# Full-height tiles for the last keys, and a gated layer whose product is read where TensorE left it

## Chip, cores and metric

One core of one Trainium2 chip runs the kernel. The metric is device time in microseconds (us) of one launch, the lower the better.

## The reference, cut to what matters

Three layers follow one another, all in float32: sliding-window attention, a gated layer with a three-tap convolution, and a second gated layer with a five-tap one.

```python
# attention: batch 4, 8 heads, 576 positions, 64 wide; window of 128 keys
scores = where((rel >= 0) & (rel < 128), q @ k.T / 8 + bias, -1e9)
attn   = softmax(scores);   x = attn @ v              # -> (4, 576, 512)
# first gated layer, taps over positions k = -1, 0, 1
h = relu(x @ w_in);         g = h * sigmoid(conv3(h)) # 1024 channels
y = g @ w_out                                         # -> (4, 576, 512)
# second gated layer, causal, five taps
gate = sigmoid(conv5(y))
out  = (gate * (y @ w_val)) @ w_out2
```

## The kernel before

Activations stand with channels on the 128 partitions and positions along the free axis. Each batch is cut into two units of positions, u=0 (positions 0 to 253) and u=1 (254 to 575), so there are eight units. A unit goes through `attention` (four pairs of heads) and then through four dense steps: `hidden` (w_in, taps, gate), `mixed` (w_out, the product called y in the reference, and its five taps), `valued` (w_val, times the gate) and `output` (w_out2, to HBM). In order to keep float32 accuracy every operand is split into a high part and a low part, and each dense product is three matmuls: high by high, low by high, high by low (`prod`, lines 693 to 695). A dense group writes one PSUM bank; the ring `ps_m` ("pm" in rows) has four banks, and for the first 16 groups only two of them, because the other two serve the widening of the weights.

In `attention` the product of the probabilities and v (line 653, written to `psx`) works on tiles of 128 keys. The two heads of a pair stand in the two 64-column halves of the array, so matmuls come in pairs, one per head. For u=1 the keys end at 576, so the last tile has only 64 keys: `half` is true there, and `kp` is 64 in place of 128. The value array in HBM is padded with zeros to 640 keys, and the probability tile `p` has its unused places set to zero once. One attention of u=1 has 30 such matmuls: three parts (high by high, high by low, low by high) of five pairs each; one of u=0 has 12. In batch 0 the three parts are issued in two groups (the two parts with high probabilities, then the third), later in one.

In `mixed`, ScalarE (ACT) copies the product from PSUM to an SBUF tile `t` (line 754, a row of line 346), `split` makes the high part (line 337 on ACT or 339 on POOL) and the low part (POOL, line 368), and the first tap is a scaling (line 346 or 347) to a tile `gts`, to which VectorE (DVE) adds four more taps (line 353). In batch 0 one of these is done by ACT (line 363) and POOL (line 364). In `hidden` the taps already read the product from its PSUM bank; rows name them `t<-pm`, those of `mixed` `gts<-t`.

The order of the instructions on each engine is not that of the source. `Program` holds every operation with an estimated duration and a priority, and a list scheduler (`forward`, `backward`, `order`) simulates the five engines seven times and writes out the order of the shortest simulated run. With `bank=` given, it keeps a second engine from an operation on a PSUM bank while another works there; with `port=` it stretches operations of DVE and POOL that overlap. `drain` marks the products with v, after which it adds 85 ns to the next matmul. An estimate that is changed changes the written order everywhere.

Of the kernel before, what the change touches and what calls it, by code (L numbers as in the profile page):

```python
# [7 lines left out]
F32 = mybir.dt.float32  # L8
# [4 lines left out]
AF = mybir.ActivationFunctionType  # L13
ALU = mybir.AluOpType
PSUM = bass.MemoryType.PSUM

B, H, S, D = 4, 8, 576, 64
# [202 lines left out]
def act_t(n, psum=False, ap=0):  # L220
    return n * 0.833 + (50 if psum else 93) + 93 * ap


def dve_t(n, ap=0, fast=False):
    return n * (0.52 if fast else 1.04) + 68 + 61 * ap
# [10 lines left out]
def mm_t(n):  # L236
    return n * 0.444 + 5.0
# [7 lines left out]
def attention_moe_moe_kernel(  # L245
# [14 lines left out]
    nc = tc.nc  # L260
    pg = Program()
# [9 lines left out]
    def st(name, shape, dt):  # L271
        return sb.tile(shape, dt, name=name)
# [15 lines left out]
    cc = st("cc", [128, KF * 3 + KD * 5], F32)  # L288
    c1 = cc[:, 0:KF * 3].rearrange("p (m k) -> p m k", k=3)
    c2 = cc[:, KF * 3:KF * 3 + KD * 5].rearrange("p (m k) -> p m k", k=5)  # L290
# [10 lines left out]
    ring_t = Ring("t", 9, [128, XMAX], F32)  # L301
# [34 lines left out]
    def cast(src, hi, n, prio, reads, writes, mode=None):  # L336
        engs = {"ACT": (act_t(n), lambda: nc.scalar.activation(out=hi, in_=src, func=AF.Copy)),  # L337
                "DVE": (dve_t(n, fast=True), lambda: nc.vector.tensor_scalar(hi, src, 1.0, 0.0, op0=ALU.mult, op1=ALU.add)),
                "POOL": (pool_t(n), lambda: nc.gpsimd.tensor_scalar(hi, src, 1.0, 0.0, op0=ALU.mult, op1=ALU.add))}  # L339
        use = tuple(mode or ('POOL', 'ACT'))  # L340
        pg.add(use, tuple(engs[e][0] for e in use), tuple(engs[e][1] for e in use), prio, reads, writes, port=True)

    def scaled(out, in_, scale, n, prio, reads, writes, engs, psum=False, bank=None):

        ap = 0 if isinstance(scale, float) else 1
        how = {"ACT": (act_t(n, psum, ap), lambda: nc.scalar.activation(out=out, in_=in_, func=AF.Copy, scale=scale)),  # L346
               "DVE": (dve_t(n, ap, fast=not psum), lambda: nc.vector.tensor_scalar(out, in_, scale, None, op0=ALU.mult) if ap
                       else nc.vector.tensor_scalar(out, in_, scale, 0.0, op0=ALU.mult, op1=ALU.add))}
        pg.add(tuple(engs), tuple(how[e][0] for e in engs), tuple(how[e][1] for e in engs), prio, reads, writes,
               bank=bank, port=not psum)  # L350
# [139 lines left out]
    def attention(b, u, p, prio, step):  # L490
# [4 lines left out]
        t0 = k0 // 2  # L495
        tiles = list(range(t0, (j0 + nb - 1) // 2 + 1))
        qk_t, qk = ring_qk.next()
        vr, vrk = V0[p] if V0 and b == u == 0 else ring_vr.next()
        v, vk = ring_v.next()
# [6 lines left out]
        if not (V0 and b == u == 0):  # L506
            sync(lambda: nc.sync.dma_start(
                out=vr[:, 0:nv], in_=vN[b, :, p, t0:t0 + nv, :]),
                early + 11052.0, (), (vrk,), 182.0 * nv)
        half = 128 * (tiles[-1] + 1) > S  # L510
        vkeys = (vrk,)
        vin, v1, v2 = vr[:, 0:nv], v[:, 0, 0:nv], v[:, 1, 0:nv]
        n = 128 * nv
# [19 lines left out]
        if turn:  # L533
            pt, ptk = ring_pt.next()
        groups = [[0, 1], [2, 3]] if nb == 4 else [[0, 1], [2, 3], [4]]
        for gi, g in enumerate(groups):
            gp, sk = ps_s.next()
            a, e = g[0], g[-1] + 1
            pr = prio + step * (e - 1)
# [10 lines left out]
            for i, s, nkey, _ in blk:  # L550
                pg.add("DVE", 128 + 1.05 * nkey, lambda i=i, s=s, nkey=nkey: nc.vector.tensor_tensor_reduce(  # L551
                    out=s, in0=s, in1=bm[:, p, 192 - nkey:192], op0=ALU.add, op1=ALU.min,
                    scale=-0.125, scalar=3.0e38, accum_out=stt[:, 0, i:i + 1]), pr, ("bm",), ((sk, i - a), (stk, 0, i)), bank=sk)
            for i, s, nkey, _ in blk:
                to, tok = s, ()
                if turn:
# [3 lines left out]
                    out=to, in_=s, func=AF.Exp, scale=-1.0, bias=stt[:, 0, i:i + 1],  # L560
# [10 lines left out]
            if turn:  # L571
                slots = []
                for i, s, nkey, _ in blk:
# [14 lines left out]
                s0, sn, st_ = slots[0], len(slots), (slots[1] - slots[0] if len(slots) > 1 else 1)  # L588
# [5 lines left out]
                    out=lo, in0=src, in1=hi, op=ALU.subtract), pr, ((sk, 0), (sk, 1), (ptk, 0, gi)), ((ptk, 1, gi),), bank=sk)  # L594
                continue
            for i, s, nkey, _ in blk:
# [4 lines left out]
                if nth_a in (31,):  # L601
                    t, tk = ring_t.next()
                    t = t[:, 0:nkey]
                    pg.add("ACT", act_t(nkey, True, 1), lambda i=i, s=s, t=t: nc.scalar.activation(
                        out=t, in_=s, func=AF.Copy, scale=stt[:, 2, i:i + 1]), pr, ((sk, i - a), (stk, 2, gi)), (tk,), bank=sk)
                    cast(t, hi, nkey, pr, (tk, "pz" + pk[1:]), ((pk, 0, i),))
                    pg.add("POOL", pool_t(nkey, True), lambda t=t, hi=hi, lo=lo: nc.gpsimd.tensor_tensor(
                        out=lo, in0=t, in1=hi, op=ALU.subtract), pr, (tk, (pk, 0, i), "pz" + pk[1:]), ((pk, 1, i),))
                    continue
                pg.add("ACT", act_t(nkey, True, 1), lambda i=i, s=s, hi=hi: nc.scalar.activation(  # L610
                    out=hi, in_=s, func=AF.Copy, scale=stt[:, 2, i:i + 1]), pr, ((sk, i - a), (stk, 2, gi), "pz" + pk[1:]), ((pk, 0, i),), bank=sk)
                pg.add("DVE", dve_t(nkey, 1), lambda i=i, s=s, hi=hi, lo=lo: nc.vector.scalar_tensor_tensor(  # L612
                    out=lo, in0=s, scalar=stt[:, 2, i:i + 1], in1=hi, op0=ALU.mult, op1=ALU.subtract),
                    pr, ((sk, i - a), (stk, 2, gi), (pk, 0, i), "pz" + pk[1:]), ((pk, 1, i),), bank=sk)
        ca, ce = (1, 8) if u == 0 else (0, 10)
        pr = prio + step * nb
        if not turn:
            pt, ptk = ring_pt.next()
# [14 lines left out]
        mms = []  # L633
        for (pq, pv) in parts:
            for t in tiles:
                for (s0, (so, no), (si, ni), oc, oo, oi) in plan[t]:
                    kp = 64 if (half and t == tiles[-1]) else 128
                    for h in range(2):
                        mms.append((pq, pv, t - t0, s0, so, no, si, ni, oc, oo, oi, kp, h))
        last = {h: max(i for i, m in enumerate(mms) if m[-1] == h) for h in range(2)}  # L640
        first = {h: min(i for i, m in enumerate(mms) if m[-1] == h) for h in range(2)}

        def do_pv(ms):
            r = []
            for i, (pq, pv, ti, s0, so, no, si, ni, oc, oo, oi, kp, h) in ms:
                base = pt[0:kp, pq].rearrange("p a c -> p (a c)")
                lhs = v[0:kp, pv, ti, 64 * h:64 * h + 64]
                o = xp[64 * h:64 * h + 64, :]
                rhs = bass.AP(base.tensor, base.offset + 128 * s0 + 64 * h,
                              [list(base.ap[0])] + [[128 * st_, n_] for st_, n_ in ((so, no), (si, ni)) if n_ > 1] + [[1, 64]])  # L650
                oap = bass.AP(o.tensor, o.offset + oc,
                              [list(o.ap[0])] + [[st_, n_] for st_, n_ in ((oo, no), (oi, ni)) if n_ > 1] + [[1, 64]])
                r.append(nc.tensor.matmul(out=oap, lhsT=lhs, rhs=rhs, start=(i == first[h]), stop=(i == last[h]),  # L653
                                          skip_group_check=True))
            return r

        for gr in ((((0, 0),), ((0, 1),), ((1, 0),)), (((0, 0), (0, 1)), ((1, 0),)), (((0, 0), (0, 1), (1, 0)),))[
                1 if b == 0 else 2]:
            ms = [(i, m) for i, m in enumerate(mms) if m[0:2] in gr]
            dur = sum(64 * m[5] * m[7] / 2.4 + 27 for _, m in ms if m[-1] == 0) + 7  # L660
            rd = tuple((ptk, q, gi) for q in sorted({g[0] for g in gr}) for gi in range(len(groups))) + tuple((vk, q + 1) for q in sorted({g[1] for g in gr}))
            pg.add("PE", dur, lambda ms=ms: do_pv(ms), pr, rd, (xpk,)).drain = True
        x, xk = ring_x.next()
# [9 lines left out]
        else:  # L673
# [3 lines left out]
                out=xl, in0=xp[:, 0:n], scalar=s_dn, in1=xh.bitcast(F32), op0=ALU.mult, op1=ALU.subtract),  # L677
                pr, (xpk, (xk, 0), (sck, 2)), ((xk, 1),))
        xkeys = ((xk, 0), (xk, 1), (xk, 2))
        if u == 1:  # L680
            _, _, pxk, px = X[b, 0, p]
# [27 lines left out]
    def split(src, hi, lo, n, sk, dk, prio):  # L709
        cast(src, hi, n, prio, (sk,), dk[0])  # L710
        sub(src, hi, lo, n, prio, (sk,) + dk[0], dk[1])
# [30 lines left out]
    def mixed(b, u, prio, rate):  # L742

        (g0, g1), (o0, o1) = GR[u], OR[u]
        Ng, No, d = g1 - g0, o1 - o0, o0 - g0
        Y[b, u] = []
        for m in range(KD):
            pr = prio + m * 3 * KF * mm_t(Ng) * rate
            yp, ypk = dense("out", m, G[b, u], Ng, pr)
            y, key = ring_g.next()  # L750
            yf, yk = ring_t.next()
            t, tk = ring_gt.next()
            yh, yl, yk2 = y[:, 0, 0:Ng], y[:, 1, 0:Ng], (((key, 0),), ((key, 1),))
            scaled(yf[:, 0:Ng], yp[:, 0:Ng], 1.0, Ng, pr, (ypk,), (yk,), ('ACT',), True)
            split(yf[:, 0:Ng], yh, yl, Ng, yk, yk2, pr)
            scaled(t[:, 0:No], yf[:, d:d + No], c2[:, m, 4:5], No, pr, (yk, "cc"), (tk,), ('ACT', 'DVE'))
            for k in range(3, -1, -1):
                lo_ = 4 - k if o0 == 0 else 0
                tap(t[:, lo_:No], yf[:, d + lo_ + k - 4:d + No + k - 4], c2[:, m, k:k + 1], No, pr, (yk, "cc"), tk,
                    k in ((3,) if b == 0 else ()))  # L760
            pg.add("ACT", act_t(No), lambda t=t: nc.scalar.activation(out=t[:, 0:No], in_=t[:, 0:No], func=AF.Tanh, scale=0.25),
                   pr, (), (tk,))
            Y[b, u].append((yh[:, d:d + No], yl[:, d:d + No], yk2[0] + yk2[1], t, tk))
        return prio + KD * 3 * KF * mm_t(Ng) * rate
# [49 lines left out]
    for p in range(NP):  # L814
        attention(0, 0, p, p * T0 / NP, T0 / NP / 5)
# [10 lines left out]
    def attentions(b, u, base, T):  # L826
        nb = len(BLK[u])
        for p in range(NP):
            attention(b, u, p, base + T * (p / NP * 0.72 + 0.081), T * 0.72 / NP / (nb + 1))
# [12 lines left out]
    t, todo = T0, UNITS  # L842
    for i, (b, u) in enumerate(todo):
        base = t
        for f in steps:
            t = f(b, u, t, rate)
# [84 lines left out]
```

## Time and profile before

| what | us |
|---|---|
| three timed runs, median (lowest to highest) | 459.61 (458.53 to 460.18) |
| the profiled execution, its own time | 460.59 |
| span of its trace, first to last instruction | 458.8 |
| TensorE (PE) busy | 444.5 (97%) |
| VectorE (DVE) busy | 351.8 (77%) |
| ScalarE (ACT) busy | 323.9 (71%) |
| GpSimd (POOL) busy | 247.8 (54%) |

The profiled execution lies 1.8 us above its span, and 1.0 us above the median. Busy time is the time in which at least one instruction of the engine was under way. The durations of matmuls overlap, so that their cost is read from the starts of two that follow one another, not from the duration of one. The granted TensorE clock is 1.0 in all of the span.

### The profile page before, as it was taken

The page shows a single profiled execution, that of the slowest core. Times are in us where ns is not written, and L with a number is a line of the kernel's source. Part 1 is how long each engine was busy: PE and PEld are TensorE (multiplying, and loading weights), DVE is VectorE, ACT ScalarE, POOL GpSimd, SP SyncE. Part 2 cuts the span into 40 slices and gives each one's busy share as a digit, 9 for nine tenths or more (in the row PEclk, how much of TensorE's full clock was granted, in tenths as well). Part 3 has the DMA queues.
Part 4 walks back from the last instruction along what each step waited for, and adds up shares of the span by engine and source line. Part 5 has one row for each costly group of instructions (what it writes and reads, how often), then busy time and mean ns, then how long its engine had stood idle before and what let it go on. Part 6 is the DMA issues. An engine that isn't in the chain of part 4 may idle for free.

```text
span 458.8 us, 10275 instructions
## 1 busy us (share of the span) xinstructions
PE 444.5 (97%) x3585; PEld 416.4 (91%) x3585; DVE 351.8 (77%) x1019; ACT 323.9 (71%) x938; POOL 247.8 (54%) x402
## 2 busy tenths in 40 slices
PE   7988999999999999999999999999999999999996
PEld 6767889988999999999999999998999999989996
DVE  5798998897997768885979487956968687936490
ACT  3988999865986568675975587766856687657532
POOL 2787889992567426340665337351753266654532
PEclk9999999999999999999999999999999999999999
DMA  8766666339643436558172427293426547460001
GB/s 271 264 221 217 212 209 214 99 94 317 146 102 60 105 89 150 116 118 182 52 131 72 108 87 164 74 183 98 68 55 136 131 106 145 81 105 1 1 1 58
DMA packets 75236, 57.86 MB, mean 126 GB/s; under 512 B 55984, under 2 KB 65968, under 8 KB 75184
## 3 DMA queue, kind: packets, MB, share of 16 engines
q1 hardware_dynamic: 75184, 57.21, 48.5%
q8 instruction: 28, 0.46, 0.4%
q14 instruction: 24, 0.20, 0.1%
HBM read 39.10 MB, written 4.72 MB: 96 GB/s over the span
## 4 chain that ended last, share of the span: by engine, by line
PE 43%; DVE 18%; ACT 13%; DMA 9%; POOL 6%; issue 3%; SPq 0%; ACTq 0%; POOLq 0%; DVEq 0%
PE pm L693 12%; PE pm L694 12%; PE pm L695 11%; DVE gts L353 7%; PE pss L547 4%; PE psx L653 4%; DMA pt<-p 3%; DMA raw<-in_w_out 3%; DVE t L353 2%; POOL g L368 2%; DMA vr<-in_vN 2%; ACT pss L559 2%; ACT p L610 1%; ACT sg L390 1%; ACT t L346 1%
## 5 line engine op out<-in xcount | busy, mean ns | idle before, releaser
L368 POOL TENSOR_TENSOR g<-t,g 128x254 fp32r<-128x254 f32 (+1 forms) x96 | 80.7, 842 | 25.5 <-ACT g L337 21.1
L353 DVE SCALAR_TENSOR_TENSOR gts<-t,cc,gts 128x322 f32<-128x322 f32 (+4 forms) x120 | 78.4, 682 | 10.4 <-ACT gts L346 8.7
L693 PE MATMUL pm<-x,win 128*128 128x256 f32 (+1 forms) x256 | 80.6, 315 | 1.1 <-DVE t L353 0.6
L693 PE MATMUL pm<-g,wout 128*128 128x254 f32 (+1 forms) x256 | 79.7, 311 | 0.0
L694 PE MATMUL pm<-x,win 128*128 128x256 f32 (+1 forms) x256 | 76.2, 298 | 0.2 <-DVE x L676 0.2
L694 PE MATMUL pm<-g,wout 128*128 128x254 f32 (+1 forms) x256 | 76.2, 298 | 0.0
L695 PE MATMUL pm<-g,wout 128*128 128x254 f32 (+1 forms) x256 | 75.8, 296 | 0.0
L695 PE MATMUL pm<-x,win 128*128 128x256 f32 (+1 forms) x256 | 75.8, 296 | 0.0
L353 DVE SCALAR_TENSOR_TENSOR t<-pm,cc,t 128x325 f32<-128x325 f32 (+3 forms) x112 | 56.0, 513 | 11.6 <-ACT t L346 9.0
L339 POOL TENSOR_SCALAR g<-t 128x254 fp32r<-128x254 f32 (+1 forms) x55 | 26.1, 474 | 69.0 <-DVE t L353 34.1
L551 DVE CUSTOM_DVE_ANT_0 pss<-pss,bm 128x192 f32<-128x192 f32 (+2 forms) x144 | 47.8, 337 | 16.3 <-PE pss L547 14.6
L547 PE MATMUL pss<-qk 128*128 128x192 f32 (+2 forms) x288 | 57.6, 323 | 2.6 <-DVE pt L593 2.6
L693 PEld LDWEIGHTS pm<-x,win 128*128 128x128 f32 x256 | 48.2, 188 | 4.4 <-DVE t L353 2.3
L559 ACT ACTIVATE pss<-pss,st 128x192 f32<-128x192 f32 (+2 forms) x108 | 40.6, 376 | 15.3 <-DVE st L551 14.0
L693 PEld LDWEIGHTS pm<-g,wout 128*128 128x128 f32 x256 | 48.2, 188 | 1.4 <-DVE t L353 0.3
L547 PEld LDWEIGHTS pss<-qk 128*128 128x128 f32 x288 | 44.8, 193 | 5.0 <-DVE pt L593 4.5
L612 DVE SCALAR_TENSOR_TENSOR p<-pss,st,p 128x192 f16<-128x192 f32 (+2 forms) x103 | 36.5, 386 | 16.1 <-DMA pt<-p 10.8
L694 PEld LDWEIGHTS pm<-x,win 128*128 128x128 f32 x256 | 48.3, 189 | 0.4 <-DVE x L676 0.4
L695 PEld LDWEIGHTS pm<-g,wout 128*128 128x128 f32 x256 | 48.6, 190 | 0.0
L694 PEld LDWEIGHTS pm<-g,wout 128*128 128x128 f32 x256 | 48.5, 190 | 0.0
L695 PEld LDWEIGHTS pm<-x,win 128*128 128x128 f32 x256 | 48.2, 188 | 0.0
L346 ACT ACTIVATE t<-pm 128x254 f32<-128x254 f32 (+2 forms) x64 | 25.8, 409 | 26.9 <-PE pm L695 26.9
(109 smaller groups left out, 1184.9 us busy)
## 6 DMA issues: line engine op xcount, KB each, us to landing
qk<-in_qk SPq DMA_DIRECT2D x16, 544.0 KB, 3.8
qk<-in_qk SPq DMA_DIRECT2D x16, 384.0 KB, 3.6
raw<-in_w_out SPq DMA_DIRECT2D x12, 512.0 KB, 4.2
raw<-in_w_in SPq DMA_DIRECT2D x8, 512.0 KB, 4.4
vr<-in_vN SPq DMA_DIRECT2D x16, 256.0 KB, 2.9
raw<-in_vN SPq DMA_DIRECT2D x8, 384.0 KB, 4.5
out<-t SPq DMA_DIRECT2D x16, 161.0 KB, 1.9
raw<-in_w_val SPq DMA_DIRECT2D x4, 512.0 KB, 3.9
```

The costliest lines, as they stand in the source:

```text
L339: "POOL": (pool_t(n), lambda: nc.gpsimd.tensor_scalar(hi, src, 1.0, 0.0, op0=ALU.mult, op1=ALU.add))}
L346: how = {"ACT": (act_t(n, psum, ap), lambda: nc.scalar.activation(out=out, in_=in_, func=AF.Copy, scale=scale)), "DVE": (dve_t(n, ap, fast ...
L353: pg.add("DVE", dve_t(n, 0 if isinstance(scalar, float) else 1), lambda: nc.vector.scalar_tensor_tensor(out=out, in0=in0, scalar=scalar, i ...
L368: "POOL": (pool_t(n, True), lambda: nc.gpsimd.tensor_tensor(out=lo, in0=src, in1=hi.bitcast(F32), op=ALU.subtract))}
L547: return [nc.tensor.matmul(out=o, lhsT=q_t[:, i, :], rhs=k_t[:, kc:kc + nkey], start=True, stop=True, skip_group_check=True) for i, o, nke ...
L551: pg.add("DVE", 128 + 1.05 * nkey, lambda i=i, s=s, nkey=nkey: nc.vector.tensor_tensor_reduce(out=s, in0=s, in1=bm[:, p, 192 - nkey:192], ...
L559: pg.add("ACT", act_t(nkey, True, 2), lambda i=i, s=s, to=to: nc.scalar.activation(out=to, in_=s, func=AF.Exp, scale=-1.0, bias=stt[:, 0, ...
L612: pg.add("DVE", dve_t(nkey, 1), lambda i=i, s=s, hi=hi, lo=lo: nc.vector.scalar_tensor_tensor(out=lo, in0=s, scalar=stt[:, 2, i:i + 1], in ...
L653: r.append(nc.tensor.matmul(out=oap, lhsT=lhs, rhs=rhs, start=(i == first[h]), stop=(i == last[h]), skip_group_check=True))
L693: return [nc.tensor.matmul(out=o, lhsT=wh, rhs=hi, start=first, stop=False), nc.tensor.matmul(out=o, lhsT=wh, rhs=lo, start=False, stop=Fa ...
L694: nc.tensor.matmul(out=o, lhsT=wh, rhs=lo, start=False, stop=False),
L695: nc.tensor.matmul(out=o, lhsT=wl, rhs=hi, start=False, stop=last)]
```

## The change

Two edits are made in the body of the kernel, and the durations that the scheduler is told follow them. First, the last tile of keys is multiplied at its full height of 128 rows: `half` and `kp` go, and the 64 upper rows hold the padding's zeros. Second, `mixed` no longer copies y out of PSUM. ACT casts the high part directly from the bank, DVE (no longer POOL) subtracts it from the bank's content for the low part, and the scaling and the taps read the bank, which therefore stays taken until the last tap.

```diff
-        half = 128 * (tiles[-1] + 1) > S
...
-                    kp = 64 if (half and t == tiles[-1]) else 128
...
-                base = pt[0:kp, pq].rearrange("p a c -> p (a c)")
-                lhs = v[0:kp, pv, ti, 64 * h:64 * h + 64]
+                base = pt[:, pq].rearrange("p a c -> p (a c)")
+                lhs = v[:, pv, ti, 64 * h:64 * h + 64]
...
-            dur = sum(64 * m[5] * m[7] / 2.4 + 27 for _, m in ms if m[-1] == 0) + 7
+            dur = sum(64 * m[5] * m[7] / 2.4 + 2 for _, m in ms if m[-1] == 0) + (120 if len(gr) > 1 else 60)
...
-            yf, yk = ring_t.next()
+            yf, yk = yp, ypk
...
-            scaled(yf[:, 0:Ng], yp[:, 0:Ng], 1.0, Ng, pr, (ypk,), (yk,), ('ACT',), True)
-            split(yf[:, 0:Ng], yh, yl, Ng, yk, yk2, pr)
-            scaled(t[:, 0:No], yf[:, d:d + No], c2[:, m, 4:5], No, pr, (yk, "cc"), (tk,), ('ACT', 'DVE'))
+            pg.add("ACT", act_t(Ng, True), lambda yf=yf, yh=yh: nc.scalar.activation(out=yh, in_=yf[:, 0:Ng], func=AF.Copy),
+                   pr, (yk,), yk2[0], bank=yk)
+            scaled(t[:, 0:No], yf[:, d:d + No], c2[:, m, 4:5], No, pr, (yk, "cc"), (tk,), ('ACT', 'DVE'), True, yk)
+            pg.add("DVE", dve_t(Ng), lambda yf=yf, yh=yh, yl=yl: nc.vector.tensor_tensor(
+                out=yl, in0=yf[:, 0:Ng], in1=yh.bitcast(F32), op=ALU.subtract), pr, (yk,) + yk2[0], yk2[1], bank=yk)
...
                 tap(t[:, lo_:No], yf[:, d + lo_ + k - 4:d + No + k - 4], c2[:, m, k:k + 1], No, pr, (yk, "cc"), tk,
-                    k in ((3,) if b == 0 else ()))
+                    k in ((3,) if b == 0 else ()), yk)
```

## Rows read from the trace of the kernel before

**Rows 1.** The page's engine table: busy us, share of span, instructions.

```profile
PE 444.5 (97%) x3585; PEld 416.4 (91%) x3585; DVE 351.8 (77%) x1019; ACT 323.9 (71%) x938; POOL 247.8 (54%) x402
```

**Rows 2.** Three stretches: busy us (instructions) of PE, PEld, DVE, ACT, POOL; granted clock.

```profile
60.00:90.00 30.00, 29.56 (x266) 27.08 (x266) 27.13 (x66) 29.77 (x76) 28.61 (x40) 1.00 0.53 179
180.00:210.00 30.00, 30.00 (x289) 28.56 (x289) 23.18 (x71) 19.56 (x61) 11.14 (x21) 1.00 0.61 131
210.00:240.00 30.00, 30.00 (x232) 28.21 (x231) 24.59 (x80) 24.44 (x75) 13.73 (x22) 1.00 0.49 110
```

**Rows 3.** PE's waits, longest first: us in total, times, longest us.

```profile
PE pss L547 <- DVE pt L593: 2.6, 6, 0.8
```

**Rows 4.** Line 653's matmuls by shape: busy us, mean ns.

```profile
L653 PE MATMUL psx<-pt,v 64*64 64x64 f16 x96 | 10.4, 213 | 0.0
...
L653 PE MATMUL psx<-pt,v 128*64 128x64 f16 x96 | 9.4, 193 | 0.0
```

**Rows 5.** PE in order of time around one product with v of u=1.

```profile
191.19 1.62 PE L653 MATMUL psx<-pt,v 128*64 128x128 f16 x30
192.75 0.39 PE L693 MATMUL pm<-g,wout 128*128 128x254 f32 x1
```

**Rows 6.** The same product: line 653's matmuls started by each window's end.

```profile
190.99:191.28 0.29, 0.09 (x4) 0.09 (x6) 1.00 0.00 0
190.99:191.39 0.40, 0.20 (x6) 0.20 (x8) 1.00 0.00 0
190.99:191.45 0.46, 0.26 (x8) 0.26 (x8) 1.00 0.00 0
190.99:191.57 0.58, 0.38 (x10) 0.31 (x10) 1.00 0.00 0
190.99:191.72 0.73, 0.53 (x12) 0.42 (x12) 1.00 0.00 0
```

**Rows 7.** PE in order of time around one product with v of u=0.

```profile
254.10 0.69 PE L653 MATMUL psx<-pt,v 128*64 128x256 f16 x12
254.72 0.42 PE L693 MATMUL pm<-g,wo 128*128 128x322 f32 x1
```

**Rows 8.** The last u=1 product, after a late weight load, counted as in rows 6.

```profile
409.80:411.21 1.41, 1.28 (x25) 1.10 (x27) 1.00 0.70 233
409.80:411.29 1.49, 1.36 (x28) 1.18 (x28) 1.00 0.71 240
```

**Rows 9.** The page's costliest groups: busy us, mean ns, idle before.

```profile
L368 POOL TENSOR_TENSOR g<-t,g 128x254 fp32r<-128x254 f32 (+1 forms) x96 | 80.7, 842 | 25.5 <-ACT g L337 21.1
L353 DVE SCALAR_TENSOR_TENSOR gts<-t,cc,gts 128x322 f32<-128x322 f32 (+4 forms) x120 | 78.4, 682 | 10.4 <-ACT gts L346 8.7
L353 DVE SCALAR_TENSOR_TENSOR t<-pm,cc,t 128x325 f32<-128x325 f32 (+3 forms) x112 | 56.0, 513 | 11.6 <-ACT t L346 9.0
L339 POOL TENSOR_SCALAR g<-t 128x254 fp32r<-128x254 f32 (+1 forms) x55 | 26.1, 474 | 69.0 <-DVE t L353 34.1
L346 ACT ACTIVATE t<-pm 128x254 f32<-128x254 f32 (+2 forms) x64 | 25.8, 409 | 26.9 <-PE pm L695 26.9
```

**Rows 10.** Single forms: busy us, mean ns, idle before.

```profile
L593 DVE TENSOR_TENSOR pt<-pss,pt 128x512 f16<-128x512 f32 x12 | 8.2, 680 | 0.4 <-ACT pt L591 0.4
...
L593 DVE TENSOR_TENSOR pt<-pss,pt 128x256 f16<-128x256 f32 x8 | 3.3, 416 | 0.1
```

**Rows 11.** Batch 0's first `mixed` (u=0): ns least, median, most; first and last start.

```profile
L695 PE MATMUL pm<-g,wout x32: 277/280/284, 70.5 to 85.9; 128*128 128x254 f32 x32
```

**Rows 12.** The last unit's end in order of time: DVE, then POOL [its idle time].

```profile
442.01 1.01 DVE L347 TENSOR_SCALAR gts<-t,cc 128x322 f32<-128x322 f32 x1
442.94 2.87 DVE L353 SCALAR_TENSOR_TENSOR gts<-t,cc,gts 128x322 f32<-128x322 f32 x6
...
446.60 1.37 DVE L776 SCALAR_TENSOR_TENSOR gts<-gts,pm 128x322 f32<-128x322 f32 x3
...
446.80 2.57 POOL L368 TENSOR_TENSOR g<-gts,g 128x322 fp32r<-128x322 f32 x3 [3.96 <-ACT g L337]
```

More of the change, by code (lines that the diff above doesn't have):

```diff
@@ L636, in attention @@
                 for (s0, (so, no), (si, ni), oc, oo, oi) in plan[t]:
-                    kp = 64 if (half and t == tiles[-1]) else 128
                     for h in range(2):
-                        mms.append((pq, pv, t - t0, s0, so, no, si, ni, oc, oo, oi, kp, h))
+                        mms.append((pq, pv, t - t0, s0, so, no, si, ni, oc, oo, oi, h))
         last = {h: max(i for i, m in enumerate(mms) if m[-1] == h) for h in range(2)}
@@ L644, in do_pv @@
             r = []
-            for i, (pq, pv, ti, s0, so, no, si, ni, oc, oo, oi, kp, h) in ms:
-                base = pt[0:kp, pq].rearrange("p a c -> p (a c)")
-                lhs = v[0:kp, pv, ti, 64 * h:64 * h + 64]
+            for i, (pq, pv, ti, s0, so, no, si, ni, oc, oo, oi, h) in ms:
+                base = pt[:, pq].rearrange("p a c -> p (a c)")
+                lhs = v[:, pv, ti, 64 * h:64 * h + 64]
                 o = xp[64 * h:64 * h + 64, :]
```

## Prediction

> **What bounds the kernel now.** I read the engine table first: TensorE is busy for 444.5 us of the 458.8, the next engine, DVE, for 351.8 [rows 1]. A busy share can hide overlap, so the stretches come next. From 180 to 240 us PE is busy in every one of the 60 us, while DVE, ACT and POOL rest for a fifth to over a half of it [rows 2]. Then the list of PE's waits: its longest entry is 2.6 us in all, over 6 waits [rows 3]. So outside the start, what is cut from PE's own issue is cut from the time, as long as the others keep up. The stretch from 60 to 90 us is different: ACT is busy for 29.77 and POOL for 28.61 of 30 us, so there it is as much these two that set the pace [rows 2].
>
> **Part one, the 64-row tile.** There are 96 matmuls of 64 rows [rows 4]: two heads by three parts in each of the 16 attentions of u=1. What one costs shows only in starts. Within a part, the pairs have 128, 256, 128, 64 and 64 columns, the last being the 64-row one. Reading the counts, the second pair has started by 191.28, the third by .39, the fourth by .45, the 64-row pair by .57 and the next part's first by .72 [rows 6]. So 256 columns took 0.11 us and 128 took 0.06, which is columns streaming; but the step into the 64-row pair took 0.12 and the step out of it 0.15, both after only 64 columns, for which a quarter of 0.11, or 0.03 us, would do. The first pair of the product, after a dense matmul, is also late in passing on: it starts at 191.19 [rows 5] and the second by .28, so 0.08 to 0.09 for 128 columns where a settled pair takes 0.06. I read the array as being emptied whenever the height of the tile changes, twice per part. A product of u=0, which has no such tile, puts 12 matmuls into 0.62 us [rows 7]; that of u=1 needs 1.56 us for 30 [rows 5].
>
> What the full-height pair will cost no row shows, and it is bounded from both sides. Below, its columns alone: 0.03 us. Above, its weights: where weights came late, three matmuls followed in 0.08 us one by one, 0.027 us each, whatever their columns [rows 8], and a pair has two loads, so 0.055 to 0.06. For the 12 products of batches 1 to 3, with three steps in and two steps out inside the product and two late first pairs spared: at the upper price 3 x (0.12 - 0.06) + 2 x (0.15 - 0.06) + 2 x 0.02 = 0.40 us; at the lower 3 x 0.09 + 2 x 0.12 + 0.04 = 0.55. The four products of batch 0 are issued in two groups, with one step out inside: 0.18 + 0.09 + 0.02 = 0.29, or 0.27 + 0.12 + 0.02 = 0.41. In all 12 x 0.40 + 4 x 0.29 = 6.0 us, or 12 x 0.55 + 4 x 0.41 = 8.2. I take 6.4, near the end that the weights give, since [rows 8] is the same instruction and narrow pairs cannot hide two loads behind so few columns.
>
> The Trainium skill speaks against this edit: TensorEngine Tiling (Array Packing), section "When to Use Tiling", has a contraction of 64 rows or fewer use two row tiles, which may double the speed. By that the sum of this part would be zero or a loss. The trace does not agree: here the partner tile is never used, and the 64-row pair is among the slowest steps of the product.
>
> **Part two, y stays in PSUM.** There are 32 tiles (8 units by 4). ACT: the copy (409 ns mean) [rows 9] becomes a cast of the same size from the same bank, so no change; the second pass for the high part goes, from ACT or from POOL (474 ns there) [rows 9]. POOL: 32 of 96 subtractions of 842 ns go [rows 9], 27 us in all, and with its share of casts some 35 of its 247.8. DVE: the 32 subtractions come to it. The nearest rows are tensor_tensor from PSUM at 416 ns for 256 columns and 680 for 512 [rows 10], so about 0.42 for the 254 columns of u=0 and 0.49 for the 326 of u=1: 14.5 us more. But the 120 taps change their source. From SBUF they take 682 ns, from PSUM, in `hidden`, 513 [rows 9]: 120 x 0.17 = 20 us less. DVE comes out some 6 us lighter. None of this is on PE's path, so I price it at nothing where PE is the bound; its cover is that DVE rests 5 to 7 us in each 30 [rows 2].
>
> A rule would turn that around. The Trainium skill, VectorE: DVE Perf Modes, section "Rules for kernel authors", advises to copy a matmul's output to SBUF first when many operations follow. Weighed against rows: the slow taps from SBUF are those that ran while POOL worked. At the end of the last unit POOL sat idle for the 3.96 us before 446.80, and there six taps took 2.87 us, 0.48 each [rows 12]. By the rule, with every SBUF tap at 0.48, the change would make DVE 120 x 0.03 + 14.5 = 18 us heavier. By rows 9, which are the mean over the whole run, it is 6 us lighter. I go by rows 9.
>
> At the end this matters. From 442 us DVE works with hardly a pause until the last gate product [rows 12], and PE's `output` waits for what follows. Two or so subtractions of 0.49 come into this queue; the scaling that took 1.01 us there [rows 12] would be near the 0.51 of a PSUM tap. I put this at +0.3 us, between -0.5 and +1.0.
>
> What is queued longer is the bank. Before, it was free after one copy of 0.41 us [rows 9]. After, it is held for the cast 0.41, the subtraction 0.42 to 0.49, the scaling about 0.5 and four taps of 0.51: 3.4 to 3.5 us plus hand-overs. With four banks the next write to it comes three groups later. One group of the first `mixed` takes (85.9 - 70.5) / 4 = 3.9 us [rows 11], so three are over 11 us: the hold is covered. But for the first 16 groups there are two banks, and the slack is one group, 3.9 us. Batch 0's extra ACT and POOL step (one SBUF addition on POOL, 0.84 like the subtraction) in the middle of the taps takes 0.4 more than the tap it replaces and two more hand-overs, so the hold reaches about 4 us there, just the slack. What stalls is the third and fourth group of `mixed` and the first two of `valued`: 0 to 1 us each, so 0 to 4. Against that stands relief in the same stretch, where POOL and ACT were full: 4 x 0.84 us of subtractions and four casts of 0.47 go, 5 us of work off two crowded engines, of which at most half is on the path. I take -0.5 for this stage, between +4 and -2.5.
>
> **Sum.** -6.4 + 0.3 - 0.5 = -6.6. The profiled execution of 460.59 us would become 454.0; it was 1.0 above the median of the runs, 459.61, which becomes 453.0.
>
> **Rivals.** (1) Part of what PE gains is given back: the freed time shows a wait on DVE or ACT, which are 5 to 10 us from full in each 30 [rows 2]. For: a list-scheduled order is written anew everywhere. Half of part one lost leaves -3.4: 456.2. Chance 0.16. (2) Relief pays more than I count: columns alone set the narrow pairs (8.2) and the crowded start gains 2.5: -10.4, or 449.2. Chance 0.08. (3) Slower: the bank's hold decides. If DVE serves taps late, each of the 32 groups keeps PE from its next bank. From 0.2 us each the gain of 6.4 is gone; at 0.4 us each the kernel is 32 x 0.4 - 6.6 = 6.2 slower: 465.8. Against: three groups of slack outside the start, and `hidden` already works from its banks with half the matmuls per group. Chance 0.05. (4) The change of height is not the reason, and narrow pairs are simply slow: every 64-column pair in the trace stands next to a change of height, so no row separates them. Then part one is worth nothing and the time is 459.4, no change. Against: the pair after the step out is late by 0.02 to 0.03 again, as after a dense matmul, which width does not explain. [...] Chance 0.06.
>
> **How the numbers follow.** The forecast, -4.5 to -9.0 with 453.0 as its middle, has 0.65. The likeliest case's own range is 450.6 to 455.1. For eight in ten the range takes in rival (1) and most of (2): 449.5 to 456.8. A measurement of this kernel can tell about 0.3%, 1.4 us, from no change. Faster: 0.65 + 0.16 + 0.08 = 0.89; same: rival (4), 0.06; slower: 0.05.
>
> **What would show it.** No 64-row matmuls in line 653; a u=1 product that lasts 1.1 to 1.2 us in place of 1.56; taps of `mixed` named gts<-pm at about 0.51 us; POOL near 213 us and DVE near 346 busy; PE busy about 438. Part one is wrong if the narrow pairs still step at 0.12 or more. Part two is wrong if PE shows waits of over 3 us in total on DVE or ACT operations on a pm bank, above all between 70 and 100 us, or if the last unit ends more than 1 us later after its last `mixed` matmul than before.

## Result

The changed kernel takes 455.37 us (median of 4 runs, 454.31 to 455.83) against 459.52 (458.53 to 460.18): ratio 0.9902, 95% interval 0.9878 to 0.9927. It is 4.2 us faster; the prediction was 453.0, 6.6 faster. The result lies 0.3 us above the likeliest case's own range (450.6 to 455.1) and inside the wider one (449.5 to 456.8). The profiled execution is the fastest of the four, 454.31, with a span of 452.5 (before 458.8), so the two traces stand 6.3 us apart, more than the medians.

The page of the changed kernel, its engine table, to be held against [rows 1]:

```profile
PE 436.9 (97%) x3605; PEld 412.1 (91%) x3605; DVE 342.7 (76%) x1056; ACT 319.9 (71%) x930; POOL 201.9 (45%) x341
```

PE is still the busiest engine, with 7.6 us less. DVE lost 9.1 us and POOL 45.9.

PE in order of time around a product with v of u=1, the counterpart of [rows 5]:

```profile
190.44 1.04 PE L651 MATMUL psx<-pt,v 128*64 128x128 f16 x30
191.41 0.76 PE L546 MATMUL pss<-qk 128*128 128x192 f32 x3
```

Thirty matmuls pass in 0.97 us; before it was 1.56. The same product as in [rows 6], with the matmuls started by each window's end in the first bracket and the weight loads in the second:

```profile
190.24:190.64 0.40, 0.20 (x6) 0.20 (x8) 1.00 0.90 361
190.24:190.69 0.45, 0.25 (x8) 0.25 (x10) 1.00 0.92 369
190.24:190.72 0.48, 0.28 (x10) 0.28 (x12) 1.00 0.91 365
190.24:190.75 0.51, 0.31 (x12) 0.31 (x14) 1.00 0.86 343
```

The third pair has started by 190.64, the fourth by .69, the fifth by .72 and the sixth, the next part's first, by .75. So the step after 128 columns takes 0.05 us and a step after 64 columns 0.03, and the steps of 0.12 and 0.15 are gone. The loads show what a change of height did: here two loads are always ahead of the matmuls, while in [rows 6] none is ahead at the step into the 64-row pair (8 and 8) or at the step out of it (10 and 10). The groups of line 651 by shape, as in [rows 4]:

```profile
L651 PE MATMUL psx<-pt,v 128*64 128x64 f16 x192 | 10.9, 194 | 0.0
```

No 64-row form is left; its 96 matmuls have joined the 96 of 128 rows and 64 columns. And the page's groups for the second edit, against [rows 9]:

```profile
L368 POOL TENSOR_TENSOR g<-t,g 128x254 fp32r<-128x254 f32 (+1 forms) x64 | 51.9, 814 | 28.2 <-ACT g L337 25.5
...
L353 DVE SCALAR_TENSOR_TENSOR gts<-pm,cc,gts 128x322 f32<-128x322 f32 (+4 forms) x120 | 57.2, 506 | 0.1
```

The 120 taps take 506 ns each from PSUM, 682 before from SBUF, and a third of POOL's subtractions has gone to DVE, where the forms show:

```profile
L755 DVE TENSOR_TENSOR g<-pm,g 128x326 fp32r<-128x326 f32 x16 | 7.8, 489 | 5.2 <-ACT gts L346 4.3 <-ACT g L752 0.9
...
L755 DVE TENSOR_TENSOR g<-pm,g 128x254 fp32r<-128x254 f32 x16 | 6.6, 410 | 0.0
```

### The profile page after: what moved, and what is told of

It is laid out like the page before. It is cut to its first block, busy times and chain, and to the rows that moved or that the text cites. A ratio compares the mean times of both kernels' runs of the same rounds, so it can differ in the third digit from the quotient of the medians.

```text
span 452.5 us, 10277 instructions
## 1 busy us (share of the span) xinstructions
PE 436.9 (97%) x3605; PEld 412.1 (91%) x3605; DVE 342.7 (76%) x1056; ACT 319.9 (71%) x930; POOL 201.9 (45%) x341
## 4 chain that ended last, share of the span: by engine, by line
PE 59%; DVE 15%; ACT 13%; DMA 7%; issue 4%; POOL 1%; SPq 0%; DVEq 0%; ACTq 0%; POOLq 0%
PE pm L691 17%; PE pm L692 15%; PE pm L693 15%; PE pss L546 5%; DVE gts L353 4%; PE psx L651 4%; DMA pt<-p 3%; DVE t L353 2%; ACT sg L390 2%; DMA raw<-in_w_in 2%; DVE pss L550 1%; ACT pss L558 1%; PE pss L584 1%; ACT pm L392 1%; DMA raw<-in_w_val 1%
## 5 line engine op out<-in xcount | busy, mean ns | idle before, releaser
L368 POOL TENSOR_TENSOR g<-t,g 128x254 fp32r<-128x254 f32 (+1 forms) x64 | 51.9, 814 | 28.2 <-ACT g L337 25.5
L563 POOL TENSOR_SCALAR st<-st 128x2 f32<-128x2 f32 (+1 forms) x56 | 11.1, 199 | 103.6 <-ACT pss L558 87.8
L353 DVE SCALAR_TENSOR_TENSOR gts<-pm,cc,gts 128x322 f32<-128x322 f32 (+4 forms) x120 | 57.2, 506 | 0.1
L611 DVE SCALAR_TENSOR_TENSOR p<-pss,st,p 128x192 f16<-128x192 f32 (+1 forms) x103 | 36.4, 386 | 12.8 <-DMA pt<-p 9.0
L609 ACT ACTIVATE p<-pss,st 128x192 f16<-128x192 f32 (+1 forms) x103 | 35.9, 403 | 14.0 <-DMA pt<-p 10.2
```

What stands on the lines that cost most here:

```text
L353: pg.add("DVE", dve_t(n, 0 if isinstance(scalar, float) else 1), lambda: nc.vector.scalar_tensor_tensor(out=out, in0=in0, scalar=scalar, i ...
L368: "POOL": (pool_t(n, True), lambda: nc.gpsimd.tensor_tensor(out=lo, in0=src, in1=hi.bitcast(F32), op=ALU.subtract))}
L563: "POOL": (165, lambda a=a, e=e: nc.gpsimd.tensor_scalar(stt[:, 2, a:e], stt[:, 1, a:e], 1e-9, 1.0 / PSC, op0=ALU.add, op1=ALU.mult))}
```

## Experiments

The changed kernel has three things in it: the height of the tile, y in PSUM, and a new estimate for the scheduler. Twelve kernels took them apart. All ratios are against runs of the kernel before on the same chip. The scheduler simulates seven orders (passes) and writes out the one with the shortest simulated span; "passes" below are counted from one, and the simulated span is the scheduler's own number.

| kernel | height | PSUM | estimate | pass, simulated us | median us | ratio (95%) |
|---|---|---|---|---|---|---|
| before | | | old | 4th, 434.2 | 459.4 (459.1 to 459.7 by chip) | 1 |
| e1 | x | | old | 4th, 434.2 | 453.95 | 0.9890 (0.9871 to 0.9909) |
| e2 | x | | new | 7th, 432.5 | 461.63 | 1.0059 (1.0036 to 1.0081) |
| e3 | | x | old | 2nd, 434.6 | 458.08 | 0.9971 (0.9953 to 0.9989) |
| e4 | x | x | old | 2nd, 434.6 | 452.62 | 0.9853 (0.9825 to 0.9881) |
| changed | x | x | new | 7th, 432.5 | 455.37 | 0.9902 (0.9878 to 0.9927) |
| e5 | x | x | new | 3rd, 433.4 | 455.54 | 0.9911 (0.9882 to 0.9941) |
| e6 | x | x | new | 2nd, 436.9 | 458.10 | 0.9960 (0.9941 to 0.9979) |
| e7 | | | old | 7th, 434.6 | 463.98 | 1.0096 (1.0071 to 1.0121) |
| e8 | x | x | old in batch 0 | 2nd, 433.2 | 454.55 | 0.9894 (0.9867 to 0.9922) |
| e9 | x | | old | 7th, 434.6 | 457.33 | 0.9965 (0.9950 to 0.9981) |
| e10 | x | x | old | 5th, 438.9 | 460.41 | 1.0027 (1.0009 to 1.0046) |
| e11 | x | x | new | 6th, 433.3 | 453.68 | 0.9895 (0.9877 to 0.9913) |
| e12 | x | | old | 5th, 435.7 | 459.98 | 1.0021 (1.0001 to 1.0042) |

Before and e1, e3 and e4, e7 and e9 are pairs in which every engine gets the same operations in the same order; within a pair only the height differs.

**e1, the height alone.**

```diff
-                    kp = 64 if (half and t == tiles[-1]) else 128
+                    kp = 128
```

> The kernel before with the last key tile at 128 rows and nothing else; the scheduler is told the old durations, so the order of every engine is that of before. Theory A (PE's issue is the bound after the start, and the height change is all of the gain): the 12 products of batches 1 to 3 fall from 1.76 us of PE time, start to start, to 1.18, so 7.0 us, and those of batch 0 give at most 1.9 more in a start that other engines bound: 452 to 453 us, 1.4 to 1.6% faster. Theory B (y in PSUM carries some of the gain): less than 3 us faster here, 456.5 or more. Theory C (the order has to be written anew to use the freed time): within 1.4 us of before.

Measured: 453.95 us, 1.1% faster. Its product with v, in PE's order of time:

```profile
189.20 1.04 PE L653 MATMUL psx<-pt,v 128*64 128x128 f16 x30
190.17 0.39 PE L693 MATMUL pm<-g,wout 128*128 128x254 f32 x1
```

0.97 us again. So the height by itself is worth about 5 us, a little less than theory A said. That is no less than the whole change gave (the two intervals overlap). Theories B and C in their plain form fall.

**e2, the height and the new estimate.**

```diff
-            dur = sum(64 * m[5] * m[7] / 2.4 + 27 for _, m in ms if m[-1] == 0) + 7
+            dur = sum(64 * m[5] * m[7] / 2.4 + 2 for _, m in ms if m[-1] == 0) + (120 if len(gr) > 1 else 60)
```

> As the height alone, and the scheduler is told the new, shorter duration of the products with v, so the order is written anew. Theory A: the estimate changes the order but not the work, within 1 us of the height alone. Theory C: the new order is worth 2 us or more, either way.

Measured: 461.63, which is 7.7 us slower than e1 with the same work. All of e1's gain is lost to the order that the new estimate led to. Theory C holds in its second form: the order matters, here against the kernel.

**e3, y in PSUM alone**, the part of the diff in `mixed`, and nothing else.

> The kernel before with y kept in PSUM for the cast, the low part and the taps; the last key tile keeps its 64 rows and the estimate of the products is the old one. Theory A: DVE and POOL are off PE's path, so no difference, within 1.4 us of before. Theory B: faster by 1.5 to 4 us. The theory that the held banks give part of the gain back: slower by 2 to 3 us, with PE waiting on DVE or ACT operations on pm banks.

Measured: 458.08, 0.3% faster, at the edge of what can be told from no change; theory A's band just holds. No loss to held banks is seen: PE waits 0.8 us in all for the taps of `mixed` on a pm bank. But its order is another one too, so this number alone does not price the edit.

**e4, both edits under the old estimate.** The changed kernel with the old line for `dur`.

> The changed kernel with the old estimate for the products with v (27 ns per pair and 7, in place of 2 and 120 or 60). Theory A: within 1 us of the changed kernel, 454.5 to 456.5. Theory C: the estimate is worth 2 us or more.

Measured: 452.62, 1.5% faster than before and 2.3 us (by ratio) to 2.8 us (by median) faster than the changed kernel; theory A's band is missed. It has the lowest median of all kernels here. Against e3, its pair, the ratio falls by 0.0118, 5.4 us: the height's gain again. The start shows where it stands. Each fence is the last group of matmuls of unit 0's `output`, with the first and last start at the end of the line; kernel before, then the changed one, e3 and e4:

```profile
L695 PE MATMUL pm<-g,wo x16: 277/280/283, 98.3 to 108.1; 128*128 128x254 f32 x16
```

```profile
L693 PE MATMUL pm<-g,wo x16: 278/280/284, 99.7 to 107.9; 128*128 128x254 f32 x16
```

```profile
L695 PE MATMUL pm<-g,wo x16: 277/280/283, 98.8 to 105.4; 128*128 128x254 f32 x16
```

```profile
L693 PE MATMUL pm<-g,wo x16: 277/280/283, 97.5 to 104.1; 128*128 128x254 f32 x16
```

In e4 unit 0's last matmul starts 4.0 us earlier than before, in the changed kernel 0.2. What follows it takes 346.0 us in the trace of e4 (span 450.1) and 344.6 in that of the changed kernel (452.5). So the whole loss of the changed kernel's order against that of e4 stands in the start.

**e5, e6, e7, e11: the same kernel in another pass.** The edit, with i = 2, 1 and 5 in the changed kernel and 6 in the one before:

```diff
-            if best is None or span < best[0]:
+            if i == 2:
```

> The changed kernel, but the order written out is that of the third of the scheduler's seven simulated passes (433.4 us by its own simulation) in place of the shortest, the last (432.5). Work, shapes and estimates are the same. Theory L (the scheduler's choice among nearly equal orders is a draw, worth several us on the chip): the three passes of the changed kernel run so far and now spread over 3 us or more, and not in the order of their simulated spans. Theory S (the short estimate makes any order worse, the start above all): within 1.5 us of the changed kernel, unit 0's last matmul at 107 us or later.

> As the one before with the second pass (436.9 us by the scheduler's own simulation, 4.4 longer than the one it chose). Theory L: anywhere from 452 to 459. Theory S: slower than the changed kernel, as simulated.

> The kernel before with the order of the scheduler's last pass (434.6 us by its own simulation, 0.4 longer than the one it chose). Theory L: 1.5 us or more from before, either way. Theory S: within 1 us of before, as the simulation has it.

> The changed kernel in the order of the sixth pass (433.3 us by the scheduler's own simulation). Theory L: within 452 to 458.5, as the other three passes of it. A theory that the kept PSUM bank is worth some 3 us over a mean of orders: 455 or so.

Measured: the changed kernel in four of its orders takes 453.68, 455.37, 455.54 and 458.10; the kernel before in two of its own 459.4 and 463.98, though the simulation sees 0.4 us between these.

Theory L is missed by e5 and e6, which with the changed kernel spread over 2.7 us and follow the simulated spans; only e7 bears it out. Theory S is missed too: e7 is 4.5 us from before, unit 0's last matmul starts at 106.5 us in e5 (106.1 in e11), and not every order under the short estimate is worse, since e10, under the old one, is slower than all four. e6 is slower than the changed kernel, as it asked. e11 lies in theory L's band, and 1.3 us below the 455 of the theory about the bank. By ratio e11, the changed kernel and e5 (0.9895, 0.9902, 0.9911), which the simulation puts within 1 us, cannot be told apart.

Wherever kernels of the same operations and the same estimate differ by more than the noise, the shorter simulated span is the faster one on the chip: before and e7; e1, e9 and e12; e4 and e10; the changed kernel and e6. What the simulation has wrong is the size: 0.4 us became 4.4 (before, e7) and 3.4 (e1, e9), all by ratio, and 4.2 became 6 to 8 (e4, e10). Between two estimates its spans did not compare here: 432.5, the shortest, belongs to e2 and to the changed kernel alike, and each is slower than its counterpart under the old estimate (e1 with 434.2, e4 with 434.6).

PE's waits in e7, as in [rows 3], without the one of 2.1 us at the start that before has too:

```profile
PE pss L585 <- DVE dg L577: 2.1, 4, 0.9
PE pm L693 <- DVE t L353: 1.9, 3, 0.9
...
PE pm L694 <- POOL g L368: 1.3, 3, 0.7
```

No one wait stands out: several of 1 to 2 us in total, for DVE, POOL and (1.4) ACT, have come in place of the one of 2.6 and shorter ones of before.

**e8, the old estimate in batch 0 alone.**

```diff
-            if best is None or span < best[0]:
+            if i == 1:
...
+            if b == 0:
+                dur = sum(64 * m[5] * m[7] / 2.4 + 27 for _, m in ms if m[-1] == 0) + 7
```

> The changed kernel with the old estimate for the products of batch 0 alone and the order of the second pass, the one that the changed kernel under the old estimate took everywhere; so the order of the start is that of the run with the old estimate, and the later units are ordered under the new one. If the loss to the new estimate sits in the order of the start: unit 0 ends at 104 to 105 us as there, and the whole takes 452 to 453.5. If it sits in the later units: 455 or more with the early start.

Measured: 454.55, between the two bands. Unit 0's last matmul starts at 105.3 us in its trace, later than the 104.1 of e4, and what follows takes 347.5 us, more than in the changed kernel (344.6) under the same estimate. So this is one more order, and it doesn't divide the changed kernel's loss.

**e9, e10, e12: more orders.** e9 is e7 with `kp = 128`; e10 is e4 and e12 is e1, each with i = 4.

> The order of the kernel before's last pass, which took 464.0 us, with the height of the last key tile changed and nothing else. If the height's gain does not depend on the order: 5 to 6 us off that, 458 to 459, as in the two pairs that have one order each (before against the height alone, the PSUM edit against the changed kernel under the old estimate), 5.5 us both. If a worse order swallows it: 461 or more.

> Both edits under the old estimate, in the order of the fifth pass (438.9 us by the scheduler's own simulation; the second pass, 434.6, took 452.6 on the chip). Theory L (a draw): anywhere from 452 to 458, so less than the 4.3 us that the simulation says may show. If the simulation is right: 456.5 or more.

> The height alone under the old estimate in the order of the fifth pass (435.7 us by the scheduler's own simulation), the counterpart without y in PSUM. If the PSUM edit is worth some 3 us over a mean of orders: 456 to 461, slower than most kernels with it. If it is worth nothing: as often below 455 as above.

Measured: e9 takes 457.33, a little below its band; its ratio is 0.0131 below that of e7, 6.0 us, so the height's gain is seen in a slow order as well. e10 takes 460.41, outside of what theory L gave it: here the simulation was right, that this order is over 4 us worse than that of e4. (In eight of e10's twelve runs the granted clock was 0.993 to 0.996; the four at 1.0 have a median of 459.1, which alters nothing in this.) e12 takes 459.98, in the band of a PSUM edit worth 3 us, which one order can't prove.

With the height edit, the seven orders with y in PSUM have a mean ratio of 0.9920 (0.9853 to 1.0027), the four without it 0.9984 (0.9890 to 1.0059). The difference, 0.0064 or 2.9 us, is smaller than either spread, so it is a hint and no more.

## Why the prediction came out as it did

**Right: what bounds the kernel, and the mechanism of part one.** PE's issue is cut and the time follows. In three pairs of one order the height gives 5.1, 5.4 and 6.0 us (ratios 0.9890; 0.9971 to 0.9853; 1.0096 to 0.9965, times 459.4), each known to 0.9 to 1.5 us. Rival (4), that narrow pairs are slow by themselves, fell: the full-height narrow pairs step in 0.03 us. The Trainium skill says in TensorEngine Tiling (Array Packing), section "Key Properties", that changing the tiling mode drains the array. The trace agrees that the change costs: with one height left in the product, 0.12 and 0.15 us became 0.03. No run puts two 64-row pairs next to each other, so what such a pair costs by itself is not shown.

**Mis-sized: the price of a narrow pair.** The prediction took the end that late weights give, 0.055 to 0.06 us, and with it 0.40 us per product. Measured, it is 0.58 us (1.55 to 0.97, medians of the 12 in before and e1), a little more than columns alone give (0.55). That makes 12 x 0.58 = 7.0 us. In batch 0 the first group went from 1.04 to 0.69 us and the second from 0.52 to 0.40, so 4 x 0.46 = 1.8, where 0.29 each had been put: 8.8 in all instead of 6.4. The step that failed is the reading of [rows 8]. With 25 to 28 matmuls started by 411.21, .24, .26 and .29, those of one head are 0.05 apart (25 and 27, 26 and 28), which is the settled step for 128 columns; the 0.027 us came from the two heads running out of step, and is no price of a load. The Trainium skill, in TensorE: Matmul & The Clock Gate, section "Step-by-step: what each phase is for", has weight loads pulled ahead of matmuls in flight. The counts agree: in the settled product two loads are ahead at every step.

**Counted, but not paid: batch 0.** Of 8.8 us, 5 to 6 arrive. Where the rest went shows when the traces of a pair of one order are laid over each other. The first edited product, the first of batch 1 with u=1, and the first after batch 2's, each in before and then in e1:

```profile
57.91 1.11 PE L653 MATMUL psx<-pt,v 128*64 128x128 f16 x20
56.81 0.76 PE L653 MATMUL psx<-pt,v 128*64 128x128 f16 x20
...
181.45 1.62 PE L653 MATMUL psx<-pt,v 128*64 128x128 f16 x30
180.02 1.04 PE L653 MATMUL psx<-pt,v 128*64 128x128 f16 x30
...
330.72 0.69 PE L653 MATMUL psx<-pt,v 128*64 128x256 f16 x12
324.76 0.69 PE L653 MATMUL psx<-pt,v 128*64 128x256 f16 x12
```

e1 is 1.1 us ahead where both kernels have run the same instructions, which is chance. Over batch 0 it gains 0.3 of the 1.8 us saved there, over batches 1 and 2 4.5 of 4.6, and from there to the end 0.7 of 2.3. In e3 and e4 the three are 1.2, 2.8 and 1.9, in e7 and e9 -0.9, 6.1 and 1.7. These are single executions, but the means, 0.2, 4.5 and 1.4, say where PE was the bound: in batches 1 and 2 nearly all arrives, in batch 0, where ACT and POOL were full for a stretch [rows 2], nearly nothing. The prediction saw that stretch and yet counted 4 x 0.29 us in it.

**Right in the direction of its busy times, open in its time: y in PSUM.** DVE came out 9.1 us lighter (6 foretold), POOL 45.9 (35), and the taps at 506 ns (513). The advice of the Trainium skill, VectorE: DVE Perf Modes, section "Rules for kernel authors", to copy to SBUF first when many operations follow is not borne out here: 682 ns from SBUF, 506 from PSUM. The prediction's step of 0.48 us for a tap beside an idle POOL [rows 12] was a distance between starts, and it was held against the duration 0.51. In durations, and in the trace of before, the taps of 322 columns from SBUF took 0.54 us where POOL was busy for under a tenth of the tap (26 of them) and 1.01 where it was for over nine tenths (8). From PSUM they take 0.54 in the changed kernel, and those of `hidden` 0.55 with POOL busy or idle. So SBUF is not slow as such; it was slow beside POOL.

The bank's hold cost little that is visible. Of PE's waits in the changed kernel,

```profile
PE pss L546 <- DVE pt L592: 3.0, 6, 1.2
...
PE pm L691 <- DVE t L353: 2.0, 4, 0.9
...
PE pm L691 <- DVE gts L353: 0.2, 1, 0.2
```

the longest is in attention. On a pm bank the taps of `hidden` (t) come to 2.0 us and those of `mixed` (gts) to 0.2; all waits before a pm bank come to 2.7, under the 3 that would have shown the prediction wrong. Rival (3) fell. The end of the last unit, from the last `mixed` matmul to the last of all, took 14.7 us (434.1 to 448.8) where before it took 15.2 (439.9 to 455.1), in another order; 0.3 more was foretold. Whether the edit is worth some 0.5 us, as the prediction had it for the start, or some 3, these runs do not settle: no two of them differ in it alone and share an order.

**Missed: the estimate.** The prediction priced the third edit, the scheduler's number, at nothing, and had rival (1) for a new order that gives some back, 456.2 with 0.16. The time came out near it. Under the old estimate the two edits take 452.62, close to the 453.0 that was foretold for them; the new one leads to an order that loses 2.3 to 2.8 of it, in the start. So 453.0 against 455.37, and 453.0 against 452.62 still more, is in part luck, the sum of errors of opposite sign: part one saves more of PE's time than was priced (8.8 against 6.4), less of that arrives (5 to 6), and the order, priced at nothing, takes some back. What in the start makes one order better than another by 3 us was not found.

## What to carry to other kernels

A tile of another height in the middle of a stream of matmuls cost here about 0.1 us on the way in and 0.1 on the way out, so pad a short contraction with zeros when its partner tile would stand unused. Take a saving off the sum in a stage that other engines fill, even when the saved work is real. When a static scheduler writes the order, an edit and an order are measured together: compare kernels that share one order, or several orders of each, before an edit gets the credit or the blame. An estimate that fits the product better (0.89 us and 0.085 for the matmul behind it, against a measured 0.97; the old one said 1.21 and 0.085) led to a worse order all the same, so an order under new estimates has to be run against one under the old, and simulated spans of the two say nothing about which is faster.

## What was not expected of the hardware

Pairs of 64-column matmuls at full height follow one another in 0.03 us, two weight loads included, with the loads two ahead; at a change of height no load was ahead, and the step took 0.12 to 0.15 us. A float32 tap of 322 columns took the same 0.54 us from SBUF as from PSUM while POOL was idle, and 1.01 from SBUF while POOL worked. The same operations in orders that the simulation puts 0.4 us apart differed by 4.5 us on the chip (459.4 and 463.98), about as much as the change under study.
